# Decay by token on y instead of q, transposed rows of x in three tiles, gathers and splits earlier in each expert

## The chip, the cores and the metric

The kernel runs on one core of a Trainium2 chip. The metric is the device time of one execution in microseconds (us); smaller is better. Before the change three runs took 712.65, 709.08 and 713.63 us (median 712.65).

The engines are named as in the profile: PE is TensorE (matmuls; PEld its weight loads), DVE is VectorE, ACT is ScalarE, POOL is GpSimd, and SP is the engine whose queue issues most of the DMAs. Each engine works through its own list of instructions in order and waits where an operand isn't ready.

## The reference

Two layers follow each other. First a decaying linear attention over 4 batches, 8 heads, 768 tokens, head size 64:

```
gamma = 1 - 2 ** (-5 - head)
state = gamma * state + outer(k[t], v[t])          # one 64x64 state per batch and head
y[t]  = (q[t] @ state) / sqrt(64)
```

Its output, as 3072 rows x of 512 columns, goes through a mixture of 8 experts with two chosen per row:

```
noisy = x @ w_gate + log1p(exp(x @ w_noise)) * noise
the two largest of 8 -> softmax over these two -> weights
out[row] += weight * (relu(x[row] @ w1[e]) @ w2[e])   # w1[e]: 512x1024, w2[e]: 1024x512
```

All inputs and outputs are float32.

## The kernel before

**Attention.** The tokens are cut into 24 chunks `j` of 128 (6 per batch). Four 256 KB tiles per chunk are loaded on SP's queue: q and k with the head's dimension on the partitions, v (`in_v`) and k again (`in_kt`) with the tokens on them. The load of chunk `j + 4` is issued in the turn of chunk `j`. The decay is split into two factors: v is multiplied by gamma to a negative power of the token (`v_scale`, POOL, L328, tile `vp`), and q by gamma to the positive power times 1/sqrt(64) (`q_scale`, POOL, L336, tile `qs`; the table is `gq`). In the turn of chunk `j`, `qk(j+1)` multiplies k with `qs` (L355), `masked` puts the causal mask on it on DVE (L360, tile `am`), `y_state` (L372) and `y_mm` (L379) add up y in PSUM (`pY`), ACT copies it to SBUF (`yt`, L383), and in the next turn PE transposes it and multiplies it with the gate's weights (`x_turn`, L405). ACT copies x out of PSUM and SP writes it to `xbuf` in HBM. Between these stands the routing (DVE: `route_*`, `own_*`), which decides which rows go to which expert, and the preparation of the first expert's weights. The tables `todo`, `mid` and `first_todo` say in which chunk's turn each such step is issued.

**Precision.** The experts' matmuls run in float16 with each operand as a high and a low part, so each product takes three matmuls (L886 to L888 in the first layer, L933 to L935 in the second).

**Experts.** Each expert has a fixed capacity (`CAPS`: 832, 832, 816, 800, 800, 784, 768, 768 rows), worked in blocks of 128 rows. For each block of expert `e + 1`, while expert `e` is computed:

- `gather`: POOL issues an indirect DMA that fetches 128 rows of `xbuf` into `xg` (four buffers; L715);
- `flush`/`gate`: DVE copies the block's gate weights from `xg` (L730);
- `split`: ACT squares and sums the rows (L743), DVE works out a power of two (L746 to L748), ACT writes the high part of `xs` (L750), DVE the low part (L751; two buffers of `xs`), and SP issues a transposing DMA from `xs` into the columns of `XE[e]` (tile `xe`, L752).

The first layer, `mm1`, goes over groups of columns (rows of x): for e = 2 to 7 two halves of 416 to 384 columns, for e = 1 groups of 256, 256 and 320. In each group it runs over the 8 slices `f` of the hidden size, 12 matmuls per slice into one PSUM tile; three such tiles are in use in turn. ACT takes the high part of relu out (`hh`, L892), DVE the low part (`hl`, L895). `n` counts the slices over all groups. After the last slice `w_scale(e+1, "1")` runs, a matmul on PE (L218) over sums of squares of the next expert's `w1` that ACT has made (`w_sum`, L208, issued at the last five slices but one; `w_cast`, L214). Then come the blocks of the second layer, `mm2`, 24 matmuls of 512 columns each (a narrower tail block is packed, `mm2_tail`, L989); ACT scales the result (`ot`, L919), and POOL adds it into `out` with an indirect DMA (`put`, L924). In these blocks ACT and DVE also convert the next expert's `w1` (`w_hi` L231, `w_lo` L236).

The order on each engine is that of the program's text: the kernel is written with a manual schedule. In the second layer's loop a gather of expert `e + 1` and the put of a block take turns on POOL, and one `split` stands behind each block from the second on; the last block of `e + 1` is split at `n = 1` of expert `e + 1` itself (for e = 1 the last five blocks, at `n = 0, 2, 9, 11, 13`).

## Time and profile before

| | |
|---|---|
| runs | 712.65, 709.08, 713.63 us; median 712.65 |
| profiled execution | 709.37 us; span from its first to its last instruction 707.6 us |
| mean granted TensorE clock | 0.960 of full speed |
| PE busy | 644.0 us (91%), 5271 matmuls |
| ACT, DVE, POOL busy | 359.0, 332.2, 204.2 us |
| DMA | 113.08 MB, mean 160 GB/s |
| stages | attention to about 121 us, first expert to about 201 us, then seven experts |

How to read it: PE is the engine with the most work, so its idle stretches and its slow stretches are what can be removed. The page's busy time counts a matmul from its start to its modelled end, so matmuls overlap; the distance between the starts of two matmuls is what one costs. The granted clock is one of two levels, 2.4 GHz (1.0) or 1.2 GHz (0.5), and the mean of a stretch tells how much of it ran at the lower one.

### The profile page before, as it was taken

How to read it: one execution, taken by the hardware profiler on the slowest of the kernel's cores; microseconds unless marked ns; L12 is line 12 of the kernel's file. 1: busy time of each engine (PE TensorE's matmuls, PEld its weight loads, DVE VectorE, ACT ScalarE, POOL GpSimd, SP SyncE). 2: the span in 40 equal slices, each digit the busy share in tenths (PEclk: the TensorE clock that was granted, in tenths of full speed). 3: DMA queues.
4: the chain of work that ended last, by engine and by line, in shares of the span. 5: the costliest groups of instructions: out<-in, count | busy, mean ns of one | idle time of the engine just before them, and what ended most of it. 6: DMA issues, size and time to landing. Idle time of an engine off the chain costs nothing.

```text
span 707.6 us, 13373 instructions
## 1 busy us (share of the span) xinstructions
PE 644.0 (91%) x5271; PEld 389.3 (55%) x5271; DVE 332.2 (47%) x889; ACT 359.0 (51%) x697; POOL 204.2 (29%) x166
## 2 busy tenths in 40 slices
PE   9989769986969899799979998999699989999995
PEld 6978657555638544354435544554255446445465
DVE  4446883985337323356436234624362355246120
ACT  6444546533647337454744475547355655477121
POOL 5555650230331024201430144014400540151204
PEclk9999979998989999899989999999899999999999
DMA  9999989967347428751775176617842786186213
GB/s 314 339 368 362 363 205 297 329 150 208 77 91 195 142 43 145 107 232 31 136 115 205 44 131 125 245 30 134 117 155 94 124 136 251 31 136 91 31 15 47
DMA packets 94429, 113.08 MB, mean 160 GB/s; under 512 B 60662, under 2 KB 61820, under 8 KB 90780
## 3 DMA queue, kind: packets, MB, share of 16 engines
q1 hardware_dynamic: 82576, 85.57, 40.6%
q0 software_dynamic: 11776, 26.63, 21.3%
q8 instruction: 42, 0.69, 0.4%
q14 instruction: 23, 0.19, 0.1%
q10 hardware_dynamic: 12, 0.01, 0.0%
HBM read 72.66 MB, written 26.42 MB: 140 GB/s over the span
## 4 chain that ended last, share of the span: by engine, by line
PE 69%; DMA 14%; DVE 8%; ACT 4%; issue 3%; POOL 1%; SPq 0%; POOLq 0%; ACTq 0%; DVEq 0%
PE pH L886 11%; PE pH L887 11%; PE pH L888 11%; PE pO L933 9%; PE pO L935 9%; PE pO L934 9%; DMA xe<-xs 6%; DMA in_v<-vt 4%; DVE xs L751 2%; PE pA L355 2%; DMA xbuf<-x 2%; ACT xs L750 1%; PE pY L379 1%; ACT junk L208 1%; DMA ct<-ctab 1%
## 5 line engine op out<-in xcount | busy, mean ns | idle before, releaser
L886 PE MATMUL pH<-xe,w1h 128*128 128x384 f16 (+5 forms) x576 | 187.0, 325 | 38.9 <-DMA xe<-xs 30.5
L887 PE MATMUL pH<-xe,w1h 128*128 128x384 f16 (+5 forms) x576 | 187.1, 325 | 0.0
L888 PE MATMUL pH<-xe,w1l 128*128 128x384 f16 (+5 forms) x576 | 186.6, 324 | 0.0
L924 POOL DMA_INDIRECT out<-ot,idx x51 | 81.3, 1594 | 352.0 <-ACT ot L919 257.3
L895 DVE SCALAR_TENSOR_TENSOR hl<-pH,hh 128x384 f16<-128x384 f32 (+5 forms) x144 | 74.7, 525 | 134.4 <-ACT hh L892 133.6
L935 PE MATMUL pO<-w2h,hl 128*128 128x512 f16 x344 | 130.4, 379 | 0.0
L934 PE MATMUL pO<-w2l,hh 128*128 128x512 f16 x344 | 130.4, 379 | 0.0
L933 PE MATMUL pO<-w2h,hh 128*128 128x512 f16 x344 | 130.4, 379 | 0.0
L892 ACT ACTIVATE hh<-pH 128x384 f16<-128x384 f32 (+5 forms) x144 | 66.6, 465 | 124.7 <-PE pH L888 123.2
L886 PEld LDWEIGHTS <-w1h 128*128 128x128 f16 x576 | 58.1, 101 | 69.8 <-issue 34.0
L919 ACT ACTIVATE ot<-pO,gse 128x512 f32<-128x512 f32 x45 | 31.0, 689 | 101.9 <-PE pO L935 96.6
L887 PEld LDWEIGHTS <-w1h 128*128 128x128 f16 x576 | 57.9, 101 | 39.4 <-issue 10.0
L888 PEld LDWEIGHTS <-w1l 128*128 128x128 f16 x576 | 58.2, 101 | 33.7 <-issue 2.8
L715 POOL DMA_INDIRECT xg<-xbuf,idx x54 | 56.7, 1050 | 61.7 <-DVE idx L628 28.8
L208 ACT ACTIVATE junk<-wst 128x1024 bf16<-128x1024 f32 x64 | 67.2, 1051 | 5.9 <-DMA wst<-w 5.8
L751 DVE SCALAR_TENSOR_TENSOR xs<-xg,xup,xs 128x512 f16<-128x512 f32 (+4 forms) x54 | 45.7, 846 | 39.5 <-ACT xs L750 38.7
L935 PEld LDWEIGHTS <-hl 128*128 128x128 f16 x344 | 33.6, 98 | 40.6
L933 PEld LDWEIGHTS <-hh 128*128 128x128 f16 x344 | 33.6, 98 | 40.6 <-issue 0.4
L934 PEld LDWEIGHTS <-hh 128*128 128x128 f16 x344 | 33.6, 98 | 39.6
L750 ACT ACTIVATE xs<-xg,xup 128x512 f16<-128x512 f32 (+4 forms) x54 | 39.1, 724 | 27.8 <-DVE xup L747 24.6
L236 DVE SCALAR_TENSOR_TENSOR w1l<-wst,wsc,w1h 128x1024 f16<-128x1024 f32 x28 | 35.9, 1281 | 31.2 <-ACT w1h L231 31.2
L746 DVE TENSOR_SCALAR xp<-xss 128x1 int32<-128x1 int32 (+4 forms) x54 | 8.2, 151 | 89.6 <-ACT junk L743 89.3
(183 smaller groups left out, 787.2 us busy)
## 6 DMA issues: line engine op xcount, KB each, us to landing
wst<-w SPq DMA_DIRECT2D x28, 1024.0 KB
in_q<-qT SPq DMA_DIRECT2D x24, 256.0 KB
in_k<-kT SPq DMA_DIRECT2D x24, 256.0 KB
in_v<-vt SPq DMA_DIRECT2D x24, 256.0 KB
in_kt<-kt SPq DMA_DIRECT2D x24, 256.0 KB
xbuf<-x SPq DMA_DIRECT2D x24, 256.0 KB
out<-zero SPq DMA_DIRECT2D x6, 1024.0 KB
wst<-w SPq DMA_DIRECT2D x8, 512.0 KB
```

Of the source, the lines that this page charges most:

```text
L208: nc.scalar.activation(junk, st[:, i * 1024:(i + 1) * 1024], AF.Square, accum_out=ss[:, i:i + 1])
L715: nc.gpsimd.indirect_dma_start(out=x[:n], out_offset=None, in_=xbuf[:128 + B0 * S] if e == 0 and t < 3 else xbuf, in_offset=bass.IndirectO ...
L751: nc.vector.scalar_tensor_tensor(xs[:n, 1], x, up[:n], xs[:n, 0], op0=OP.mult, op1=OP.subtract)
L886: nc.tensor.matmul(p[:, :n], whi, xh, start=(k == 0), stop=False)
L887: nc.tensor.matmul(p[:, :n], whi, xl, start=False, stop=False)
L888: nc.tensor.matmul(p[:, :n], wlo, xh, start=False, stop=(k == KT - 1))
L892: nc.scalar.activation(hh[:, f, n0:n1], p, AF.Relu)
L895: nc.vector.scalar_tensor_tensor(hl[:, f, n0:n1], p, 0.0, hh[:, f, n0:n1], op0=OP.max, op1=OP.subtract)
L924: nc.gpsimd.indirect_dma_start(out=out, out_offset=bass.IndirectOffsetOnAxis(ap=idx[:n, i:i + 1], axis=0), in_=ot[:n], in_offset=None, com ...
L933: nc.tensor.matmul(p, a, WT["2h"][:, f, :], start=(f == 0), stop=False)
L934: nc.tensor.matmul(p, a, WT["2l"][:, f, :], start=False, stop=False)
L935: nc.tensor.matmul(p, c, WT["2h"][:, f, :], start=False, stop=(f == FT - 1))
```

## The change

- **y carries the token's factor.** `q_scale` and its tile `qs` are gone. q goes into `qk` and `y_state` as it was loaded, and where ACT copied y out of PSUM (L383), DVE now multiplies it there by the table `gq` (`yt<-pY,gq`). The table's columns are put in y's order. The buffers of q become five (three before).
- **Inputs in another order.** The first loads: v and k (`kt`) of chunk 0 come before q and k of chunk 1, and so on.
- **Weights of the first expert.** `w_sum`, `w_scale`, `w_hi` and `w_lo` of `w1` move one chunk later.
- **Three tiles for the transposed rows.** `XE[e]` becomes tiles of 384, 256 and CAPS[e] - 640 columns, and `mm1` of every expert from e = 1 on goes over these three groups (24 slices; the last group is 192 columns wide for e = 1, then 176, 160, 160, 144, 128 and 128).
- **Gathers and splits sooner.** From e = 2 on the first four gathers of `e + 1` are issued at `n = 9, 11, 13, 15` and the first four splits at `n = 13, 15, 17, 19`, the other three of each at the second layer's blocks 0 to 2 and 1 to 3. For e = 1: gathers at `n = 13, 15, 17, 19`, splits at `17, 19, 21, 23`. At the end of e = 0 three blocks are split, not two; the others in e = 1 at `n = 0, 2, 9, 11`.

```diff
     for h in range(H):
-        y[h % 2, h // 2, :] = gamma[h] ** (p + 1.0) / math.sqrt(D)
-        g[h % 2, :, h // 2] = gamma[h] ** (np.arange(NC) * float(C))
+        o, x = (h // 2 + h % 2) % 2, h % 2 * 2 + h // 4
+        y[o, x, :] = gamma[h] ** (p + 1.0) / math.sqrt(D)
+        g[o, :, x] = gamma[h] ** (np.arange(NC) * float(C))
     rest, parts = np.concatenate([y.reshape(2, HP * C), g.reshape(2, NC * HP)], 1).astype(np.float32), []
...
             IN[n, j] = loads.tile([128, HP, C] if n in "kq" else [128, DM], F32, name="in_" + n,
-                                  bufs=AHEAD + {"k": 0, "q": -1, "v": 0, "kt": 1}[n])
+                                  bufs=AHEAD + {"k": 0, "q": 1, "v": 0, "kt": 1}[n])
             nc.sync.dma_start(IN[n, j].rearrange("p a c -> p (a c)") if n in "kq" else IN[n, j], src[n][j])
...
     nc.sync.dma_start(cs, ctab[:, :SOON])
+    load(0, ("v", "kt"))
     load(1, "qk")
-    load(0, "v")
-    load(2, "q")
-    load(0, ("kt",))
-    load(2, "k")
     nc.sync.dma_start(wgf, wgn)
-    load(1, ("v", "kt"))
+    load(1, ("v",))
+    load(2, "qk")
+    load(1, ("kt",))
+    load(2, ("v", "kt"))
     for j in range(3, AHEAD):
-        load(j, "qk")
-        load(j - 1, ("v", "kt"))
-    load(AHEAD - 1, ("v", "kt"))
+        load(j)
...
-    VP, AM, QS, PY, PT, YT, LG = {}, {}, {}, {}, {}, {}, {}
+    VP, AM, PY, PT, YT, LG = {}, {}, {}, {}, {}, {}
     pctx = ExitStack()
...
-    def q_scale(j):
-        QS[j] = loads.tile([128, HP, C], F32, name="qs", bufs=3)
-        eng, m = nc.vector if j == 0 else nc.gpsimd, 2 if j < 2 else 1
-        for x in range(m):
-            r = slice(x * HP // m, (x + 1) * HP // m)
-            eng.tensor_tensor(QS[j][:, r], IN["q", j][:, r], gq[:, j % NC].rearrange("p (a c) -> p a c", a=HP)[:, r], op=OP.mult)
-
     def q_table(c):
...
-    q_scale(0)
     q_table(1)
...
                 nc.tensor.matmul(pA[s][:, i, :], IN["k", j][r, i, :],
-                                 QS[j][r, i, :], start=True, stop=True)
+                                 IN["q", j][r, i, :], start=True, stop=True)
         return pA
...
                 r = slice(s * 64, s * 64 + 64)
-                nc.tensor.matmul(yplace(j, i, s), U[c % 2][r, i, :], QS[j][r, i, :],
+                nc.tensor.matmul(yplace(j, i, s), U[c % 2][r, i, :], IN["q", j][r, i, :],
                                  start=(i < 2), stop=False, skip_group_check=True)
...
         y = YT[j].rearrange("p s g c -> p (s g c)")
-        nc.scalar.activation(y.rearrange("p (s x) -> p s x", s=2), PY.pop(j)[:, :, :2 * C], AF.Copy)
+        nc.vector.tensor_tensor(y.rearrange("p (s x) -> p s x", s=2), PY.pop(j)[:, :, :2 * C],
+                                gq[:, c].rearrange("p (s x) -> p s x", s=2), op=OP.mult)
         if c < NC - 1:
...
         o, n, i = block(e, t)
-        if t == 0:
-            XE[e] = XP[e % 2].tile([128, 2 * KT, CAP], F16, name="xe")
+        if t in (0, 3, 5):
+            w = {0: FIRST, 3: 640 - FIRST, 5: CAP - 640}[t]
+            XE[e, o] = XP[e % 2].tile([128, 2 * KT, w], F16, name=f"xe{t}")
         x = XP[0].tile([128, XROW], F32, name="xg", bufs=4)
...
             nc.vector.scalar_tensor_tensor(xs[:n, 1], x, up[:n], xs[:n, 0], op0=OP.mult, op1=OP.subtract)
-            nc.sync.dma_start_transpose(XE[e][:, :, o:o + n], xs[:n].rearrange("p a d -> p (a d)"))
+            b = (0, FIRST, 640)[(t >= 3) + (t >= 5)]
+            nc.sync.dma_start_transpose(XE[e, b][:, :, o - b:o - b + n], xs[:n].rearrange("p a d -> p (a d)"))
...
         at((4, 6, 9, 12)[i], w_load, 0, "1", i)
-        at0((6, 8, 11, 14)[i], w_sum, 0, "1", i)
-        at0(15 + i, w_hi, 0, "1", i)
+        at0((7, 9, 12, 15)[i], w_sum, 0, "1", i)
+        at0(16 + i, w_hi, 0, "1", i)
         at((20, 20, 21, 21)[i], w_load, 0, "2", i)
...
             at0(22 + i, w_sum, 0, "2", i)
-    first_todo[15].insert(0, (w_scale, (0, "1")))
-    for i, j in ((0, 16), (1, 16), (2, 17), (3, 17), (4, 18), (5, 19), (6, 20), (7, 21)):
+    first_todo[16].insert(0, (w_scale, (0, "1")))
+    for i, j in ((0, 17), (1, 17), (2, 18), (3, 18), (4, 19), (5, 20), (6, 20), (7, 21)):
         P(j, w_lo_half, 0, "1", i)
...
-    q_scale(1)
     v_scale(0)
...
             f(*a)
-        if j < 2:
-            q_scale(j + 2)
         if more:
             v_scale(j + 1)
-        if 2 <= j < NCH - 2:
-            q_scale(j + 2)
         if more:
...
             wlo = WT["1l"][:, k, f * 128:(f + 1) * 128]
-            xh, xl = XE[e][:, k, n0:n1], XE[e][:, KT + k, n0:n1]
+            xh, xl = XE[e, n0][:, k, :n], XE[e, n0][:, KT + k, :n]
             nc.tensor.matmul(p[:, :n], whi, xh, start=(k == 0), stop=False)
...
     for e in range(E):
-        half = (CAPS[e] + 31) // 32 * 16
-        cols = [(FIRST, 640), (640, CAPS[0])] if e == 0 else [(0, half), (half, CAPS[e])]
-        if e == 1:
-            cols = [(0, 256), (256, 512), (512, CAPS[e])]
+        cols = [(0, FIRST), (FIRST, 640), (640, CAPS[e])][not e:]
         n, more = 0, e + 1 < E
...
         for n0, n1 in cols:
-            if n0 and ready:
+            if n0 == FIRST and ready:
                 for t in range(ready):
...
                 mm1(e, n0, n1, f)
-                if n in ((2, 4) if e == 0 else (0, 2, 9, 11, 13) if e == 1 else (1,)):
+                if n in ((2, 4) if e == 0 else (0, 2, 9, 11, 17, 19, 21, 23) if e == 1 else (13, 15, 17, 19)):
                     split()
+                if e and ahead and n in ((13, 15, 17, 19) if e == 1 else (9, 11, 13, 15)):
+                    ahead.pop(0)()
+                    flush(2)
                 if e:
...
                     w_sum(e + 1, "2", n - 2)
-            if more and (n in (1, 2) if e == 0 else n):
+            if more and 0 < n < 4:
                 split()
```

The order of the instructions moves at three places. The first is ACT at the end of expert 3's first layer, before the change (`hh` is the high part of relu, `junk,wss` a sum of squares of the next expert's `w1`, `wsb` what `w_scale` on PE waits for):

```order
L892 ACTIVATE hh<-pH 128x400 x5
L208 ACTIVATE junk,wss_4536<-wst_4535 128x1024
L892 ACTIVATE hh<-pH 128x400
L208 ACTIVATE junk,wss_4536<-wst_4535 128x1024
...
L214 ACTIVATE wsb_4740<-wss_4536 128x4
L892 ACTIVATE hh<-pH 128x400
```

The same place now, all slices of the third group of columns (`junk,xss` and `xs` are the two ACT instructions of a split):

```order
L881 ACTIVATE hh<-pH 128x160 x2
L736 ACTIVATE junk,xss<-xg 128x512
L743 ACTIVATE xs<-xg,xup 128x512
L881 ACTIVATE hh<-pH 128x160 x2
L736 ACTIVATE junk,xss<-xg 128x512
L743 ACTIVATE xs<-xg,xup 128x512
L209 ACTIVATE junk,wss_4614<-wst_4613 128x1024
L881 ACTIVATE hh<-pH 128x160
...
L215 ACTIVATE wsb_4994<-wss_4614 128x4
L881 ACTIVATE hh<-pH 128x160
```

The four sums of squares still stand at the last slices but one; those slices are 160 columns wide now, not 400, and two of the four splits that moved forward stand before them in the same group.

The second place is DVE around chunk 15 of the attention, where the lists of the first rows are made; now (`yt<-pY,gq` is y times its table, `am` the masked scores of the next chunk, `a` and `ob` one-hot tables of the routing):

```order
L374 TENSOR_TENSOR yt<-pY,gq 128x512
L351 TENSOR_TENSOR am<-pA,mask 128x512 x2
L549 TENSOR_TENSOR a_12_1269<-lanes,lf_12_1267 128x1536
L557 TENSOR_TENSOR ob_12_1335<-blks,lf_12_1267 128x84
L559 TENSOR_TENSOR ob_12_1335<-ob_12_1335,tokn 128x84
L530 COPY cum<-pR 128x9
L531 TENSOR_SCALAR cum<-cum 128x1
L374 TENSOR_TENSOR yt<-pY,gq 128x512
L351 TENSOR_TENSOR am<-pA,mask 128x512 x2
```

Each chunk's `yt` now stands on DVE behind the routing of its turn and ahead of the next chunk's mask; before, DVE had the same rows without `yt`, and the four small instructions of `w_scale` after the two rows of `cum`.

The third place is POOL in expert 4, now (`xg<-xbuf` is a gather, `out<-ot` a put):

```order
L708 DMA xg<-xbuf,idx 128x528 x5
L913 DMA out<-ot,idx 3200x512
L708 DMA xg<-xbuf,idx 128x528
L913 DMA out<-ot,idx 3200x512
L708 DMA xg<-xbuf,idx 16x528
L913 DMA out<-ot,idx 3200x512 x5
```

Before, one gather and one put took turns through all seven blocks of the second layer. Now four gathers are through before the first put.

## Rows read from the trace of the kernel before

**Rows 1.** Busy time by engine in two stretches of the attention (columns as in the first row).

```profile
core 0: us, PE busy (x) PEld busy (x) DVE busy (x) ACT busy (x) POOL busy (x), PEclk, DMA share, GB/s
60.00:80.00 20.00, 15.26 (x318) 13.93 (x322) 17.58 (x54) 8.31 (x21) 11.64 (x9) 0.94 1.03 358
80.00:100.00 20.00, 14.79 (x336) 12.93 (x330) 17.00 (x30) 9.65 (x20) 13.98 (x12) 0.93 0.78 268
```

**Rows 2.** Groups by line and shape: busy us, mean ns | idle before.

```profile
L360 DVE TENSOR_TENSOR am<-pA,mask 128x512 f32<-128x512 f32 x48 | 30.9, 686 | 34.0 <-PE pA L355 34.0
L336 POOL TENSOR_TENSOR qs<-in_q,gq 128x512 f32<-128x512 f32 x22 | 28.4, 1292 | 31.1 <-DMA in_q<-qT 17.8 <-PE pY L372 9.5 <-PE pU L388 3.8
```

**Rows 3.** Timeline, all engines, about 91 us: start, duration, instruction.

```profile
91.46 1.05 POOL L328 TENSOR_TENSOR vp<-in_v,cs 128x512 f32<-128x512 f32 x1
91.63 5.87 DVE L751 SCALAR_TENSOR_TENSOR xs<-xg,xup,xs 128x512 f16<-128x512 f32 x1 [0.73 <-ACT xs L750]
...
95.91 1.03 POOL L328 TENSOR_TENSOR vp<-in_v,cs 128x512 f32<-128x512 f32 x1
```

**Rows 4.** Groups by line on PE: 275 to 600 us, then 195 to 245 us.

```profile
L886 PE MATMUL pH<-xe,w1h 128*128 128x400 f16 (+2 forms) x307 | 105.3, 343 | 21.0 <-DMA xe<-xs 14.1 <-issue 5.0 <-DVE hl L895 1.9
L886 PE MATMUL pH<-xe,w1h 128*128 128x256 f16 (+1 forms) x86 | 25.6, 298 | 10.6 <-DMA xe<-xs 10.5
```

**Rows 5.** Timeline of PE: two resumptions, idle time before them in brackets.

```profile
234.71 0.43 PE L886 MATMUL pH<-xe,w1h 128*128 128x320 f16 x1 [3.08 <-DMA xe<-xs]
...
581.28 0.32 PE L886 MATMUL pH<-xe,w1h 128*128 128x384 f16 x1 [1.95 <-DVE hl L895]
```

**Rows 6.** Ten us behind each resumption (columns as in rows 1).

```profile
207.30:217.30 10.00, 10.00 (x77) 8.29 (x78) 4.19 (x16) 4.79 (x11) 4.91 (x4) 0.83 0.52 80
234.70:244.70 10.00, 9.99 (x62) 6.70 (x63) 1.97 (x4) 2.80 (x7) 0.00 (x0) 0.83 0.51 201
288.70:298.70 10.00, 10.00 (x47) 5.04 (x48) 3.97 (x13) 3.49 (x7) 2.46 (x2) 0.80 0.61 102
361.90:371.90 10.00, 9.99 (x43) 4.98 (x44) 3.23 (x10) 3.82 (x9) 2.74 (x3) 0.71 0.58 102
433.10:443.10 10.00, 10.00 (x52) 5.43 (x52) 6.46 (x17) 4.53 (x10) 4.05 (x4) 0.85 0.56 93
506.50:516.50 10.00, 9.97 (x47) 5.19 (x48) 3.83 (x12) 3.96 (x9) 2.37 (x2) 0.77 0.44 89
581.30:591.30 10.00, 10.00 (x62) 6.05 (x62) 6.89 (x19) 6.18 (x9) 1.57 (x2) 1.00 0.80 266
```

**Rows 7.** Timeline of ACT, expert 0, slices of 192 columns with sums of squares.

```profile
180.34 1.06 ACT L208 ACTIVATE junk<-wst 128x1024 bf16<-128x1024 f32 x1
...
181.39 0.33 ACT L892 ACTIVATE hh<-pH 128x192 f16<-128x192 f32 x1
181.60 1.07 ACT L208 ACTIVATE junk<-wst 128x1024 bf16<-128x1024 f32 x1
```

**Rows 8.** Timeline of ACT, expert 1: from a split's first instruction to what follows it.

```profile
224.09 0.62 ACT L743 ACTIVATE junk<-xg 128x512 bf16<-128x512 f32 x1
...
225.84 0.37 ACT L892 ACTIVATE hh<-pH 128x256 f16<-128x256 f32 x1
```

**Rows 9.** Timeline, end of expert 2's first layer: `wsb` and the matmul behind it.

```profile
323.52 0.21 ACT L214 ACTIVATE wsb<-wss 128x4 bf16<-128x4 f32 x1
...
323.78 0.17 PE L218 MATMUL pR<-wsb,oneb 128*128 128x4 bf16 x1
```

**Rows 10.** Timeline of PE at the full clock: narrow matmuls, each with its own weight load.

```profile
177.41 0.32 PE L619 MATMUL pB<-ob,a 128*128 128x49 f16 x6
177.57 0.24 PE L886 MATMUL pH<-xe,w1h 128*128 128x192 f16 x1
...
178.06 0.25 PE L886 MATMUL pH<-xe,w1h 128*128 128x192 f16 x1
```

**Rows 11.** The chain of waits into expert 1: start, duration, what.

```profile
201.59 5.56 DMA xe<-xs
```

**Rows 12.** Timeline of DVE behind expert 0's last block.

```profile
203.20 0.75 DVE L993 SCALAR_TENSOR_TENSOR ot<-pT,gse,ot 64x512 f32<-64x512 f32 x1
```

## The prediction

> **What bounds the kernel now.** I read the busy times by stretch first, then the groups by line with their idle time, then the timeline where idle time is large, and last the order of ACT's instructions, because PE's waits end there. In the attention's middle the DMAs are full (share 1.03 from 60 to 80 us, 0.78 from 80 to 100) while DVE has hardly any room left (17.58 and 17.00 of 20 us) [rows 1]. So the input's volume sets the pace first and DVE's queue later; POOL and ACT have room. In the experts PE is the bound, and what can be won is its idle time ahead of the first layer: 21.0 us between 275 and 600 us, mostly waits for transposed rows, and 10.6 us around expert 1 [rows 4]. Idle time costs twice. Behind each of the longer waits the clock ran at the lower of its two levels for a while: in the ten us behind the four large waits between experts the mean was 0.80, 0.71, 0.85 and 0.77, so 2.0, 2.9, 1.5 and 2.3 us were lost, 8.7 in all [rows 6]. A wait of 1.95 us had no such cost (1.00 behind it), one of 3.08 us had (0.83) [rows 5, 6].
>
> **The waits between experts, e = 2 to 7.** The gathers and splits of the next expert now start in the first layer. The last split of `e + 1` stands behind block 3 of the seven of `e`, so three blocks of some 5 us lie between it and the first use. The whole wait goes, and with it the slow stretch: -21.0 - 8.7 = **-29.7 us**. Next in line there would be the conversion of `w1`, which is through a block or more earlier as before. The bound on the other side is that nothing goes, if the transposes are late all the same (a rival).
>
> **What ACT has to do now in the third group.** This is the price. The moved splits bring two ACT instructions each into the first layer. In the second group (256 columns) there is room. In the third the slices are 128 to 192 columns wide, and the four sums of squares of the next `w1`, tied to the last slices, stand there too. One sum of squares with one `hh` takes ACT 1.26 us, of which `hh` 0.21 [rows 7], so 1.05 without it. A split holds ACT 1.75 us from its first instruction to the next `hh`, its wait for DVE included [rows 8]. From the start of the third group in e = 2 to 6 ACT has: the `hh` and split of the slice before, 2.0; seven `hh`, some 1.4; two splits, 3.5; four sums, 4.2; and 0.26 from `wsb` to the matmul behind it [rows 9]. That is 11.4 us. PE cannot pass: `w_scale` waits on `wsb` and stands ahead of the whole second layer, and only three PSUM tiles let the slices run ahead of ACT. PE alone needs less: matmuls of 192 columns follow each other in 0.49 / 6 = 0.082 us [rows 10], which is 192 columns at 2.4 GHz and 2 ns, so 8 x 12 of them cost 7.2 us at 176 columns, 6.6 at 160, 6.0 at 144 and 5.3 at 128. The waits: 4.2, 4.8, 4.8, 5.4, 6.1, together 25.3. For e = 1 (192 columns, 7.9 us) there is no split just before, but three stand ahead of `wsb`: 2.1 for two slices, six `hh` 1.3, splits 5.25, sums 4.2 and 0.26 make 13.1, so 5.2. In all **+30.5 us**. The lower bound is half of it, if PE could use part of the wait; the upper bound adds up to 1 us per expert, because `xs` has two buffers and the third split must wait for the first one's transpose (5.56 us where others were in flight [rows 11]).
>
> **The clock behind these waits.** Each wait falls into pieces: about 2 us while PE lacks a PSUM tile, another 1, and some 2.4 before `w_scale`. One such piece lies at or above the 1.95 us that cost nothing and below the 3.08 us that cost 1.7 [rows 5, 6], but three of them stand close together. Bounds 0 and six times 1.7, 10; I take **+5**.
>
> **Expert 1's first wait.** Its first group is now 384 wide, not 256, so it needs a third block, whose split stands behind the packed tail block of expert 0. DVE finishes that tail at 203.20 + 0.75 = 203.95 [rows 12]; then come the power of two, 0.3, ACT's and DVE's part of `xs`, about 0.75 each, and a transpose of 5.56 [rows 11]: 211.3 us, where before the second block had landed at 201.59 + 5.56 = 207.2. That is +4.2. Against it the wait of 3.08 us in the middle goes, with its 1.7 of slow clock, as the last two splits stand two slices sooner and the group ahead of them is longer: **-0.6**.
>
> **More matmuls.** e = 2 to 7 have 96 more each, 576 at 2 ns: **+1.2**. At this point a row and a rule differ. Six matmuls of 49 columns, each with a load of 128x128 weights, took 0.16 us, 27 ns each [rows 10], so a weight load does not hold back a matmul of 128 columns at 55 ns. The Trainium skill (TensorE: Matmul & The Clock Gate, Back-to-back issue gap) says that a sustained stream of load and matmul pairs takes about 81 ns each at 128 columns. By that rule expert 7, where ACT has nothing else beside it, would pay, as an estimate, 96 x 26 ns = 2.5 us more, and the others nothing, since 96 x 81 ns = 7.8 us still hides behind ACT's 11.4.
>
> **Attention.** POOL loses 22 multiplies of 1.29 us [rows 2], ACT its copy; neither bounds. DVE gets 24 multiplies out of PSUM, priced like the mask, 0.69 us [rows 2]. From 60 to 80 us five of them, 3.4 us, meet 17.58 busy: 1 us over [rows 1]. In the turns with splits DVE has mask 1.3, y 0.7, two low parts of weights 1.5 and a split 1.2, 4.7 us for a turn of some 4: three turns, +2. Against it stands one instruction of DVE that took 5.87 us, not the 0.75 of its like [rows 3, 12], while POOL ran vp and `qs` without a break beside it; without `qs` there is no such run: -5.1. Sum **-2**; bounds -7 (all of y's multiplies hidden) and +8 (the stall stays on account of vp, and every y from chunk 12 on counts). The order of the first loads and the five q buffers I cost at nothing: the DMAs carry the same bytes, and nothing there waits for a q buffer.
>
> **Sum.** -29.7 + 30.5 + 5 - 0.6 + 1.2 - 2 = +4.4 on the profiled execution's 709.4: 713.8. The median shown, 712.65, lies 3.3 above that execution, so the same sum on it gives 717. I predict **715**.
>
> **Rivals.** *Even (the forecast, 0.48)*: the waits between experts move into the third group; its own range is 707 to 722.
>
> *Faster (0.2).* The clock stays up behind the pieces of wait (-5) and the attention gains its whole stall (-5 more): 704 to 707. For it: no piece alone reaches 3.08 us. Against it: DVE's 17 of 20 us [rows 1].
>
> *Slower through the clock (0.2).* The pieces act as one wait, and the slow stretch behind each is as long as the longest of rows 6, 2.9 us: six times 2.9 in place of 5 is +12.4, 726 to 729. Its place is the end of each first layer from e = 1 to 6, and it decides from the point where the pieces count like the 3.08 us of rows 5. The Trainium skill (TensorE: Matmul & The Clock Gate, A second HAM failure mode: psum-queue depth-cycling) describes a kernel in which short idle times between matmul groups, one PSUM tile after another, kept the clock going down and up. By that rule this case is the likely one; the 1.95 us with no cost speaks against it here, so I leave it at 0.2.
>
> *Slower in the attention (0.08).* DVE becomes its bound and the term is +8, not -2: 724.
>
> *The waits stay (0.04).* If the transposes queue behind the 2 MB of `w2` on SP, -29.7 falls away: 744. Against it: four of seven stand ahead of those loads, and the last has three blocks of time.
>
> **Chances and range.** One per cent, 7 us, is about what a measurement of this kernel can tell from no change. Faster by more than that (below 705.5): most of the faster rival, 0.17. Slower (above 719.8): both slower rivals, the last one and the forecast's upper edge, 0.31. Between: 0.52. The range from 701 to 728 leaves out the last rival and the tails of the others.
>
> **What would show it.** Right: no idle ahead of the first matmul of e = 2 to 7; in each third group of e = 1 to 6 PE waits 4 to 6 us, in part for ACT's `hh`, in part at `w_scale` for `wsb`; expert 1 starts later than before against the end of expert 0; no DVE instruction of 5 us near 92 us; POOL below 180 us busy. Wrong: if PE passes the third group in its own 5 to 8 us, the main price is wrong and the time falls to about 685; if the attention ends later than before, DVE's queue was underrated.

## The result and the profile after

The changed kernel takes **721.0 us** (720.0 to 722.3), the kernel before 711.1 beside it: a ratio of **1.014, 95% interval 1.009 to 1.018**. The profiled execution took 722.29 us, with a span of 720.5; before it was 709.37. The forecast was 715 in a range of 701 to 728. The time lies in the range, but above the one per cent within which I had put 0.52 of the chance: it belongs to the 0.31 for slower.

The page after: the span, each engine's busy time, and the granted clock in 40 slices of 18 us.

```profile
span 720.5 us, 14594 instructions
PE 647.5 (90%) x5847; PEld 422.6 (59%) x5847; DVE 340.5 (47%) x959; ACT 349.5 (49%) x721; POOL 174.8 (24%) x142
PEclk9999889998979999999999899989999999899999
```

The groups by line on PE answer to [rows 4]. First 195 to 245 us, then 275 to 600, then `L875` and the matmul of `w_scale` (`L219`) from 240 to 650 us, which holds all six third groups.

```profile
L875 PE MATMUL pH<-xe,w1h 128*128 128x384 f16 (+2 forms) x96 | 28.0, 292 | 10.2 <-DMA xe<-xs 9.1 <-DVE hl L884 1.1
...
L875 PE MATMUL pH<-xe,w1h 128*128 128x384 f16 (+4 forms) x435 | 119.7, 281 | 12.8 <-DVE hl L884 12.7
...
L875 PE MATMUL pH<-xe,w1h 128*128 128x384 f16 (+6 forms) x488 | 130.8, 276 | 17.4 <-DVE hl L884 17.2
L219 PE MATMUL pR<-wsb,oneb 128*128 128x4 bf16 x11 | 1.8, 166 | 15.4 <-ACT wsb L215 15.4
```

The 21.0 us of waiting between experts are gone: what ends the idle time now is `hl`, not a transpose. In their place stand 17.4 us for `hl` and 15.4 in front of `w_scale`. Expert 3's third group shows how they fall, first in PE's timeline, from the group's first matmul on (the idle time before each in brackets):

```profile
382.94 0.23 PE L875 MATMUL pH<-xe,w1h 128*128 128x160 f16 x1
...
386.41 0.23 PE L875 MATMUL pH<-xe,w1h 128*128 128x160 f16 x1 [0.70 <-DVE hl L884]
388.67 0.23 PE L875 MATMUL pH<-xe,w1h 128*128 128x160 f16 x1 [0.44 <-DVE hl L884]
393.42 0.23 PE L875 MATMUL pH<-xe,w1h 128*128 128x160 f16 x1 [2.92 <-DVE hl L884]
396.79 0.16 PE L219 MATMUL pR<-wsb,oneb 128*128 128x4 bf16 x1 [1.72 <-ACT wsb L215]
```

and in ACT's timeline, with the fourth split (the second in this group), two of the four sums and the end:

```profile
388.39 0.20 ACT L736 ACTIVATION_READ_ACCUMULATOR junk<-xg 128x1 f32 x1
391.06 0.72 ACT L743 ACTIVATE xs<-xg,xup 128x512 f16<-128x512 f32 x1 [2.47 <-DMA xe<-xs]
391.69 1.04 ACT L209 ACTIVATE junk<-wst 128x1024 bf16<-128x1024 f32 x1
392.72 0.28 ACT L881 ACTIVATE hh<-pH 128x160 f16<-128x160 f32 x1
392.91 1.04 ACT L209 ACTIVATE junk<-wst 128x1024 bf16<-128x1024 f32 x1
...
396.54 0.20 ACT L215 ACTIVATE wsb<-wss 128x4 bf16<-128x4 f32 x1
```

ACT's one long break, beside waits for DVE of 0.4 and 0.6 us in the splits, is 2.47 us in the middle of the fourth split, when it waits for an earlier transpose to give back one of the two `xs` buffers. The `hh` that PE needs stands behind both.

The ten us behind each of the six `w_scale` matmuls answer to [rows 6] (stretch, length, busy time and instructions of PE, PEld, DVE, ACT and POOL, granted clock, DMA share, GB/s).

```profile
247.00:257.00 10.00, 10.00 (x41) 4.20 (x41) 3.35 (x12) 3.23 (x6) 1.77 (x2) 0.84 0.68 210
321.30:331.30 10.00, 10.00 (x40) 4.21 (x40) 8.85 (x35) 1.82 (x3) 1.70 (x2) 0.83 0.41 169
396.80:406.80 10.00, 10.00 (x40) 4.20 (x40) 2.01 (x8) 1.86 (x3) 1.61 (x1) 0.82 0.41 170
469.70:479.70 10.00, 10.00 (x35) 3.95 (x35) 0.96 (x8) 1.80 (x3) 0.83 (x1) 0.71 0.41 172
544.30:554.30 10.00, 10.00 (x41) 4.19 (x41) 2.18 (x8) 1.78 (x3) 1.97 (x2) 0.86 0.44 171
616.90:626.90 10.00, 10.00 (x36) 3.99 (x36) 1.13 (x8) 1.78 (x3) 1.04 (x1) 0.73 0.42 175
```

PE works through every one of these stretches, and in each the clock stood at 1.2 GHz for 3 to 6 us: 1.6 + 1.7 + 1.8 + 2.9 + 1.4 + 2.7 = 12.1 us lost. In expert 3 the slow stretch begins before its window and costs 0.8 more, so 13.

In the attention, the windows that answer to [rows 1], the split that answers to the 5.87 us of [rows 3], and the group of y's new multiplication; then two waits of PE, the first in the kernel before (in front of `w_scale` of expert 0), the second in the changed one:

```profile
60.00:80.00 20.00, 18.44 (x429) 16.35 (x428) 17.06 (x63) 8.45 (x20) 4.16 (x4) 1.00 1.02 333
80.00:100.00 20.00, 13.38 (x286) 12.05 (x288) 15.43 (x48) 8.80 (x21) 8.25 (x9) 0.83 1.08 329
...
94.99 0.83 DVE L744 SCALAR_TENSOR_TENSOR xs<-xg,xup,xs 128x512 f16<-128x512 f32 x1 [0.73 <-ACT xs L743]
...
L374 DVE TENSOR_TENSOR yt<-pY,gq 128x512 f32<-128x512 f32 x24 | 16.5, 689 | 12.2 <-PE pY L370 9.3 <-ACT lgs L408 2.2 <-issue 0.6
...
77.16 0.18 PE L218 MATMUL pR<-wsb,oneb 128*128 128x4 bf16 x1 [3.75 <-DMA xbuf<-x]
...
89.81 1.34 PE L397 MATMUL pT<-turn,yt 64*64 64x80 f32 x32 [4.77 <-DVE yt L374]
```

DVE is busy for less of both stretches than before, although the multiplication is its own now; the stretches don't hold quite the same chunks, and the long instruction lay in the second only. The gain does not arise where that instruction stood. The 17th `yt` starts at 75.57 us, before the change at 82.64: 7.1 sooner already, with PE's wait of 3.75 us gone (its `w_scale` stands a chunk later now) and the three one-hot instructions of DVE beside it taking 2.2 us in all, not 4.6. Two turns later PE waits 4.77 us for DVE's `yt`, and the lead is down to 2.5 (88.98 against 91.50). Behind the long instruction it is 6.2 (95.75 against 101.90), and 5.1 at expert 0's first product.

### The profile page after: what moved, and what is told of

Read it like the earlier page. It is cut to its first block, busy times and chain, and to the rows that moved or that the text cites. A ratio compares the mean times of both kernels' runs of the same rounds, so it can differ in the third digit from the quotient of the medians.

```text
span 720.5 us, 14594 instructions
## 1 busy us (share of the span) xinstructions
PE 647.5 (90%) x5847; PEld 422.6 (59%) x5847; DVE 340.5 (47%) x959; ACT 349.5 (49%) x721; POOL 174.8 (24%) x142
## 4 chain that ended last, share of the span: by engine, by line
PE 61%; DMA 17%; ACT 7%; DVE 7%; issue 5%; SPq 1%; POOL 1%; POOLq 0%; ACTq 0%
PE pO L922 10%; PE pO L923 10%; PE pO L924 10%; PE pH L875 9%; PE pH L877 9%; PE pH L876 9%; DMA xe<-xs 5%; DMA in_k<-kT 4%; ACT junk L209 4%; DMA xbuf<-x 3%; DMA in_v<-vt 2%; DVE xs L744 2%; ACT xs L743 2%; PE pT L978 1%; DMA xg<-xbuf,idx 1%
## 5 line engine op out<-in xcount | busy, mean ns | idle before, releaser
L875 PE MATMUL pH<-xe,w1h 128*128 128x384 f16 (+6 forms) x768 | 209.5, 280 | 34.0 <-DVE hl L884 18.9
L876 PE MATMUL pH<-xe,w1h 128*128 128x384 f16 (+6 forms) x768 | 209.6, 280 | 0.0
L877 PE MATMUL pH<-xe,w1l 128*128 128x384 f16 (+6 forms) x768 | 209.4, 280 | 0.0
L884 DVE SCALAR_TENSOR_TENSOR hl<-pH,hh 128x384 f16<-128x384 f32 (+6 forms) x192 | 80.7, 433 | 127.2 <-ACT hh L881 125.4
L922 PE MATMUL pO<-w2h,hh 128*128 128x512 f16 x344 | 135.6, 394 | 0.0
L923 PE MATMUL pO<-w2l,hh 128*128 128x512 f16 x344 | 135.2, 393 | 0.0
L881 ACT ACTIVATE hh<-pH 128x384 f16<-128x384 f32 (+6 forms) x192 | 73.4, 388 | 117.0 <-PE pH L877 102.9
L876 PEld LDWEIGHTS <-w1h 128*128 128x128 f16 x768 | 75.9, 99 | 41.4 <-issue 22.8
L875 PEld LDWEIGHTS <-w1h 128*128 128x128 f16 x768 | 75.9, 99 | 38.1 <-issue 12.1
L877 PEld LDWEIGHTS <-w1l 128*128 128x128 f16 x768 | 76.0, 99 | 20.2 <-issue 0.9
L744 DVE SCALAR_TENSOR_TENSOR xs<-xg,xup,xs 128x512 f16<-128x512 f32 (+4 forms) x54 | 40.7, 754 | 44.3 <-ACT xs L743 44.3
L327 POOL TENSOR_TENSOR vp<-in_v,cs 128x512 f32<-128x512 f32 x24 | 25.3, 1054 | 65.1 <-DMA in_v<-vt 50.4
```

The costliest lines, as they stand in the source:

```text
L744: nc.vector.scalar_tensor_tensor(xs[:n, 1], x, up[:n], xs[:n, 0], op0=OP.mult, op1=OP.subtract)
L875: nc.tensor.matmul(p[:, :n], whi, xh, start=(k == 0), stop=False)
L876: nc.tensor.matmul(p[:, :n], whi, xl, start=False, stop=False)
L877: nc.tensor.matmul(p[:, :n], wlo, xh, start=False, stop=(k == KT - 1))
L881: nc.scalar.activation(hh[:, f, n0:n1], p, AF.Relu)
L884: nc.vector.scalar_tensor_tensor(hl[:, f, n0:n1], p, 0.0, hh[:, f, n0:n1], op0=OP.max, op1=OP.subtract)
```

## The experiments

The kernels ran in four groups, each on one chip beside the kernel before, whose median there was 701.7 us (x1, x8, x6, x3), 707.6 (a2, x9, c1, c2), 703.8 (x4, c6, c5) and 705.8 (c7). So ratios to it are compared between groups, not times. The forecasts in us of the first group (x1, x8, x6, x3) were made from the 711.1 us of the first result; as ratios they are these times divided by 711.1.

**x1: the sums of squares sooner.**

```
-if more and e and len(cols) * FT - 5 <= n < len(cols) * FT - 1:
-    w_sum(e + 1, "1", n - (len(cols) * FT - 5))
+s0 = 13 if e == 1 else 8
+if more and e and s0 <= n < s0 + 4:
+    w_sum(e + 1, "1", n - s0)
```

> Edit: in experts 1 to 6 the four sums of squares over the next expert's first weights stand earlier: behind slices 8 to 11 of 24 (13 to 16 in expert 1) and no longer behind slices 19 to 22, where ScalarE also makes the four splits and the narrow slices' results. Theory (ScalarE's pile-up in the third column group, and the half clock behind it, are what ate the gain): TensorE's waits in the third groups fall from 32.8 us in sum to 5 to 10, the half-clock stretches behind them (about 12 us by the stages) go nearly all: 683 to 693 us against 721 of the changed kernel. Rival 1 (the third, narrow group itself, its matmuls and weight loads, costs the time): the waits for hh and hl stay, 715 to 722. Rival 2 (the sums only move their 5 us per expert onto the second group, where the splits now begin): as much wait in front of the middle group's slices, 710 to 722.

Measured: 692.1 us, ratio 0.987 (0.981 to 0.993). PE from 240 to 650 us:

```profile
L875 PE MATMUL pH<-xe,w1h 128*128 128x384 f16 (+6 forms) x531 | 143.5, 278 | 14.8 <-DVE hl L884 14.6
L219 PE MATMUL pR<-wsb,oneb 128*128 128x4 bf16 x12 | 2.0, 168 | 0.0
```

The waits at `w_scale` go whole and moving the sums onto the second group cost nothing, so neither rival holds. But the ratio misses the theory's 0.960 to 0.975 too, and 14.8 us for `hl` stay, more than the 5 to 10 that I gave: ACT still waits 1.1 to 2.4 us for a transpose in the last splits of experts 2 to 6. Of the six slow stretches one is left.

**x8: gathers and splits where they were, three tiles kept.**

```
-if n in (... (0, 2, 9, 11, 17, 19, 21, 23) if e == 1 else (13, 15, 17, 19)):
+if n in (... (0, 2, 9, 11) if e == 1 else (1,)):
     split()
-if e and ahead and n in (...):
-    ahead.pop(0)()
-    flush(2)
...
-if more and 0 < n < 4:
+if more and (0 < n < 4 if e == 0 else n):
     split()
```

> Edit: the three tiles and three column groups stay, but from expert 1 on the gathers and splits stand where the kernel before has them (gathers and splits among the blocks of the second product; expert 1's own splits behind slices 0, 2, 9 and 11). Theory (the three tiles alone take away the wait for the last transposes at each expert's start; the earlier splits alone load ScalarE in the third group): third-group waits fall to below 10 us in sum, no idle of over 1 us in front of the first matmul of experts 2 to 7: 680 to 692 us. Rival 1 (it is the earlier gathers and splits that took the wait at the start away): the waits at the starts return, some 3 us at each expert, and the time is 700 to 712. Rival 2 (sums and narrow slices alone are too much for ScalarE in the third group): 710 to 722.

Measured: 701.7 us, ratio 0.998 (0.993 to 1.002). That is outside the theory's range (0.956 to 0.973 as a ratio) and inside that of rival 1 (0.984 to 1.001), but not by rival 1's mechanism. PE from 240 to 650 us:

```profile
L875 PE MATMUL pH<-xe,w1h 128*128 128x384 f16 (+6 forms) x515 | 139.0, 279 | 8.6 <-DVE hl L884 8.4
L219 PE MATMUL pR<-wsb,oneb 128*128 128x4 bf16 x12 | 2.0, 166 | 12.1 <-ACT wsb L215 12.1
```

No matmul of experts 2 to 7 waits for a transpose at its start, so the three tiles with their column groups alone take that wait away; the earlier splits weren't needed for it. The 8.4 us for `hl` lie in the first group, behind late splits in which ACT waits 0.7 to 2.3 us for a gather, and the sums in the narrow slices alone are worth 12.1 us at `w_scale`.

**x6: `w_scale` behind the first block of the second product.** Edit: the line `w_scale(e + 1, "1")` moved from ahead of that loop to behind its first `put`.

> Edit: the broadcast product of w_scale for the next expert's first weights, TensorE's instruction that waits for the last sum of squares, stands behind the first block of the second product and no longer ahead of it. Theory (the in-order queue of TensorE makes the sums' lateness its own wait): the six waits in front of that product (3.98, 2.31, 1.72, 2.38, 2.45 and 2.52, 15.4 us in sum) go, with half or all of the half clock behind them (6 to 12 us); the waits for hl in the third group (17 us) stay: 693 to 703 us. Rival (what is late behind it is the next step of the same chain, the halves of the next expert's weights at the end of the second product, and the next expert's first slice waits for them): 712 to 721.

Measured: 695.6 us, ratio 0.992 (0.988 to 0.996). The same two groups show 17.4 us for `hl`, as after the change, and 0.0 at `L219`: the theory's waits, and no next one behind them. The ratio lies just above the forecast's 0.975 to 0.989. In the traces the stretch from expert 1's first matmul to the span's end takes 490.9 us, after the change 516.2: 25.3 less, of which 15.4 are the waits and some 9.5 the clock, for two slow stretches (3.4 us each) are left there of the six, which cost 13. By the ratios the gain is 15 us against the first result and 21 against a2 below.

**x3 and x4: the change's two halves, each on the kernel before.** x3 takes the diff's parts up to `y_mm`, the loads' order and expert 0's later weight steps; x4 the parts from `gather` on and the column groups.

> Edit: the kernel before with the attention part of the change alone: decay on y in VectorE, no scaled q, inputs in the new order, expert 0's weight steps one chunk later; experts as before. Theory (the attention gained 5 us, as the start of expert 0's first product shows, 113.2 against 118.3 us, and the experts lost the rest): 704 to 708 us, 3 to 7 below the kernel before. Rival (VectorE's multiplication, late behind others, costs as much in a normal run, and the 5 us are one execution's chance): 710 to 714.

> Edit: the kernel before with the expert part of the change alone (three tiles and column groups, earlier gathers and splits); attention, inputs and expert 0's weight steps as before. Theory (attention gains some 4 us, as x3 showed with a ratio of 0.9944, and the experts lose more than the whole result: pile-up and half clock against the waits between experts): the ratio to the kernel before is that of the changed kernel (1.014 to 1.022) plus 0.005: 1.017 to 1.030. Rival (the two parts are not independent: y's product in VectorE is also what delays the experts): 1.000 to 1.012.

Measured: x3 698.1 us, ratio 0.994 (0.990 to 0.999); x4 728.8 us, ratio **1.037** (1.032 to 1.042), above even the theory's 1.030. So the attention gained and the experts lost, 25 us by x4's median. In the traces the stretch from expert 1's first matmul to the span's end takes 500.3 us before the change and 495.6 in x3, whose experts are the same; 516.7 in x4, and 516.2 and 516.6 in the two traces of the changed kernel. So the experts' loss is 16 to 21 us with either attention, and x4's rival falls. The two halves don't add up, though: 0.994 times 1.037 is 1.031, and the whole change has 1.014 and 1.022. x4's extra time lies ahead of expert 1, which starts at 209.7 us there, at 207.3 before, and at 204.3 and 200.5 in the changed kernel; how much of it is the chip stays open. In the two traces with the old attention (before, x4) the first product of expert 0 starts at 118.3 and 117.8 us, in the twelve with the new one at 109.0 to 113.2, mean 110.9: a gain of 7, where the pair that I read first gave 5.1.

**a2: the change again.** No edit.

> The changed kernel itself once more, because x1, x3, x6 and x8 ran on a chip on which the kernel before takes 701.7 us and not 711: its ratio to the kernel before there is needed beside theirs. If its 1.0138 is the change's own, the ratio is 1.008 to 1.018, its third-group waits sum to 30 to 35 us again, and all six are followed by a half-clock stretch. If instead the third-group waits cost the clock less on this chip than in the first execution (in x6, on that chip, only two of six waits for hl were followed by one), the ratio is 0.995 to 1.007.

Measured: 719.7 us, ratio 1.022 (1.014 to 1.029). The waits are the same (16.9 for `hl`, 14.8 at `w_scale`), and all six have a slow stretch behind them. The loss is the change's own. Why it is 1.014 on one chip and 1.022 on the other isn't settled; the waits that the change removes differ too (31.6 us ahead of the first products from 195 us on in the first trace of the kernel before, 26.1 in x3).

**x9: the waits filled.**

```
+def fill(e, n):
+    for _ in range(FILL.get((e, n), 0)):
+        nc.tensor.matmul(pR[:, :FIRST], WT["1h"][:, 0, :128], XE[e, 0][:, 0, :FIRST], ...)
...
+                fill(e, n)
                 mm1(e, n0, n1, f)
...
+            fill(e, 24)
             w_scale(e + 1, "1")
```

> Edit: the changed kernel with extra products of 384 columns (0.16 us each) whose result nobody reads, put in front of the third-group slices and of the w_scale products at which TensorE was seen to wait over 1 us, each batch shorter than the wait it stands in: 20.5 us of TensorE's idle filled, no wait taken away. Theory (the half clock behind the six waits is a cost of its own, some 12 us in the changed kernel's trace): the half-clock stretches at the end of the third groups go, all or nearly all, the waits' ends stay where they were, and the time is 6 to 13 us below the changed kernel's in the same call. Rival (the waits alone are the cost, and the half clock runs while TensorE has to wait anyhow): within 3 us of the changed kernel, or above it by what the extra products overrun.

Measured: 709.2 us, ratio 1.004 (1.000 to 1.008), 10.5 us below a2. PE's groups from 240 to 650 us (`L1094` is the filling), and three of the six windows behind `w_scale`, the others alike:

```profile
L875 PE MATMUL pH<-xe,w1h 128*128 128x384 f16 (+6 forms) x513 | 138.5, 278 | 8.4 <-DVE hl L884 8.2
L1094 PE MATMUL pR<-xe,w1h 128*128 128x384 f16 x137 | 24.4, 326 | 0.0
L219 PE MATMUL pR<-wsb,oneb 128*128 128x4 bf16 x12 | 2.0, 166 | 2.6 <-ACT wsb L215 2.5
...
246.90:256.90 10.00, 10.00 (x48) 4.57 (x48) 3.35 (x12) 3.21 (x6) 2.63 (x2) 1.00 0.69 201
463.00:473.00 10.00, 9.71 (x48) 4.43 (x46) 2.24 (x9) 2.84 (x6) 2.32 (x2) 1.00 0.54 202
606.80:616.80 10.00, 10.00 (x48) 4.58 (x48) 2.16 (x8) 1.82 (x3) 2.63 (x2) 1.00 0.56 187
```

137 useless products of 0.16 us were added, 22 us of work, and the kernel got faster: the clock reads 1.00 behind all six. No wait was taken away, only filled: from a third group's first matmul to the `w_scale` matmul behind it the six experts take 77.2 us in sum, 78.1 in a2. From expert 1's first matmul to the span's end it takes 503.4 us against 516.6 in a2: 13.2 us, about what the six half-clock stretches cost there (14.1). The rival falls.

**c1: everything early.** Splits behind slices 5, 7, 8 and 10, sums behind 9, 11, 12 and 13, gathers behind 1 to 4, for experts 2 to 6 (the copies of the gate weights, `flush`, move with them).

```
-(13, 15, 17, 19)     +(5, 7, 8, 10)      split
-(9, 11, 13, 15)      +(1, 2, 3, 4)       gather
+sums = (13, 14, 15, 16) if e == 1 else (9, 11, 12, 13)
```

> Edit: in experts 2 to 6 all work for the next expert stands in the first two column groups: gathers behind slices 1 to 4, splits behind 5, 7, 8 and 10, sums of squares behind 9, 11, 12 and 13 (expert 1: sums behind 13 to 16, the rest as changed). Theory (only what ScalarE must do in the third group costs anything there): the third-group waits fall to below 4 us in sum, from some 33 in the changed kernel and 13 to 16 in x1, with no wait at the experts' starts either: 6 to 13 us below x1, a ratio of 0.968 to 0.980 to the kernel before. Rival (ScalarE or VectorE is then late in the first two groups, for hl): as x1, 0.983 to 0.992.

Measured: 727.9 us, ratio **1.034** (1.026 to 1.041). The theory falls, and the rival's range is left far behind too, though its mechanism is what is seen: PE waits 41.9 us in this group, 14.8 in x1. That line (240 to 650 us), two of PE's waits in expert 4's second group, and ACT's instructions there:

```profile
L875 PE MATMUL pH<-xe,w1h 128*128 128x384 f16 (+6 forms) x483 | 131.5, 282 | 41.9 <-DVE hl L884 26.9 <-DVE xp L739 14.9
...
456.58 0.27 PE L875 MATMUL pH<-xe,w1h 128*128 128x256 f16 x1 [1.00 <-DVE xp L739]
459.89 0.27 PE L875 MATMUL pH<-xe,w1h 128*128 128x256 f16 x1 [1.85 <-DVE xp L739]
...
454.32 0.62 ACT L736 ACTIVATE junk<-xg 128x512 bf16<-128x512 f32 x1
454.84 0.19 ACT L736 ACTIVATION_READ_ACCUMULATOR junk<-xg 128x1 f32 x1
456.80 0.72 ACT L743 ACTIVATE xs<-xg,xup 128x512 f16<-128x512 f32 x1 [1.77 <-DVE xup L740]
457.43 0.36 ACT L881 ACTIVATE hh<-pH 128x256 f16<-128x256 f32 x1
```

A split goes from ACT to DVE and back. With low parts of weights in DVE's queue (1.28 us each) it held ACT 3.1 us here, not the 1.75 of [rows 8], and a slice of 256 columns takes PE 1.3.

**c2: c1 with expert 0's border mended.** The load of expert 1's second weights (2 MB) stands behind slice 3 of expert 0's second group, not ahead of it; its splits behind slices 1 and 3; expert 1's first three splits before, behind, and before the second of expert 0's last blocks.

> Edit: c1, and around expert 0: the load of expert 1's second weights (2 MB) behind slice 3 of expert 0's second group and no longer ahead of it, the splits there behind slices 1 and 3, and expert 1's first three splits ahead of, behind, and ahead of the second of expert 0's blocks of the second product. Theory: the wait in front of expert 0's third group (7.4 us in x1, where a transpose issued at 157.2 us landed 11.7 us later beside 4 MB of weights) falls to 2 to 4, the one in front of expert 1 (8.65 us in x1, its third split behind two results and a gather's copy) to 0 to 3, with part of the half clock behind them (10 us of it behind each in x1, at a loss of 5): 10 to 18 us below c1. Rival (the transposes wait for something else that ends as late, the gathers' landings or expert 1's weight parts): 0 to 4 us below c1.

Measured: 713.1 us, ratio 1.011 (1.004 to 1.018), 15 below c1, as the theory said. PE's group from 155 us on, c1 first (to 210 us), then c2 (to 200):

```profile
L875 PE MATMUL pH<-xe,w1h 128*128 128x192 f16 (+2 forms) x56 | 16.4, 293 | 15.2 <-DMA xe<-xs 14.9 <-DVE hl L884 0.3
...
L875 PE MATMUL pH<-xe,w1h 128*128 128x192 f16 (+2 forms) x67 | 18.8, 281 | 2.0 <-DMA xe<-xs 1.2 <-DVE hl L884 0.5 <-DVE xp L739 0.3
```

**c6 (x1 with c2's steps) and c5.** c5 is x8 with x1's sums and c2's steps, and with an expert's last three splits behind slices 1, 5 and 7 of its own first group (gate copies and output scales move with them).

```
-(0, 2, 9, 11) if e == 1 else (1,)       +(0, 2, 9, 11) if e == 1 else (1, 5, 7)
-(0 < n < 4 if e == 0 else n)            +(n == 0 if e == 0 else 0 < n < 5)
```

> Edit: x1 (sums of squares early, splits as changed) with c2's steps around expert 0 (second weights' load behind a slice, splits one slice sooner, expert 1's first three splits around the first blocks). Theory: x1's ratio of 0.987 less the 15 us that the same steps took off between c1 and c2: 0.962 to 0.972. Rival (the steps only gained there because c1 had other waits behind them): 0.980 to 0.988.

> Edit: x8 (gathers and splits among the blocks of the second product) with x1's early sums, with the last three of the seven splits of an expert moved from the end of the second product to behind slices 1, 5 and 7 of the first group, where ScalarE has room between two results of 384 columns, and with c2's steps around expert 0. Theory (a piece of ScalarE's work costs nothing where TensorE's slice is longer than that piece and the slice's own result together, 1.92 us a slice in the first group against 1.28 in the second): no wait of over 1 us in experts 2 to 6, 0.945 to 0.962. Rival (the last splits still wait for gathers that land late, as at 420.4 us in x8, and hold up hh): 0.962 to 0.975, no better than c6.

Measured: c6 672.6 us, ratio **0.957** (0.952 to 0.962), better than forecast. PE's group from 240 to 650 us, and the stretch from 190 to 640:

```profile
L875 PE MATMUL pH<-xe,w1h 128*128 128x384 f16 (+5 forms) x576 | 153.0, 275 | 13.7 <-DVE hl L884 13.6
...
190.00:640.00 450.00, 434.69 (x2964) 264.92 (x2963) 202.41 (x548) 250.21 (x495) 116.65 (x87) 1.00 0.56 128
```

The waits for `hl` in the third groups are nearly those of x1, and the clock stays whole behind all of them.

c5 took 670.4 us, ratio **0.954** (0.948 to 0.960). Its time is in the theory's range, but not its picture: at the border of the first two groups PE waits 2.65 us for `hl` in four experts, for DVE's share of the seventh split and the output scales.

**c7: c5 with the seventh split and the scales a little later.** Split behind slice 9, scales behind 10, sums behind 11 to 14.

> Edit: c5 with the seventh split of experts 2 to 6 behind slice 9 and no longer behind slice 7, the output scales (three short VectorE operations that need it) behind slice 10, and the sums of squares behind slices 11 to 14. Theory (the 2.65 us that TensorE waits for hl at the border of the first two groups in experts 2 to 5 of c5 is VectorE's queue: a split's part, the scales, and the last low part of the second weights, all between slices 7 and 8): these waits and the 3.4 us half-clock stretch behind three of them go, 10 to 15 us below c5, 0.930 to 0.942 of the kernel before. Rival (the same work in the shorter slices of the second group makes the same wait there, as in c1): 0.950 to 0.962, as c5.

Measured: 659.5 us, ratio **0.944** (0.937 to 0.952): just above the forecast's 0.942, and below c5 by 0.010, some 7 us, not 10 to 15. It beats both kernels. Three things moved at once in c7, so which of them counts isn't shown.

```profile
L875 PE MATMUL pH<-xe,w1h 128*128 128x384 f16 (+5 forms) x576 | 152.4, 276 | 0.5
...
200.00:300.00 100.00, 99.36 (x720) 65.19 (x719) 52.64 (x149) 57.72 (x117) 20.64 (x16) 1.00 0.58 144
300.00:400.00 100.00, 99.90 (x645) 56.80 (x644) 45.19 (x120) 61.28 (x116) 33.42 (x27) 1.00 0.66 136
400.00:500.00 100.00, 99.80 (x742) 64.15 (x741) 48.31 (x125) 58.97 (x120) 20.89 (x17) 1.00 0.59 146
500.00:600.00 100.00, 99.89 (x649) 57.12 (x647) 46.55 (x120) 63.35 (x120) 28.94 (x22) 1.00 0.65 129
```

From 240 to 650 us the group waits 0.5 us where it waited 17.4, and the clock is whole throughout. ACT and DVE do the same work as in the changed kernel; only its order differs.

## Why the prediction came out as it did

- **Waits between experts, -29.7: right.** Not one is left at the start of experts 2 to 7, nor the slow stretch behind. x8 adds that the three tiles with their column groups do this alone. The size is that of one execution: in x3, with the same experts, these waits sum to 16.2 us, not 21.0.
- **ACT in the third group, +30.5: right in place, 8 too small.** PE's rows show 17.4 + 15.4 = 32.8, in the two kinds foretold; x1 and x6 take the `w_scale` part away and x8 most of the other. But from the third group's first matmul to `w_scale` the six experts take 13.5, 12.7, 13.8, 12.4, 13.0 and 12.5 us (expert 3: 382.94 to 396.79), 38.2 more than PE's own work as I reckoned it. The sums of ACT's work, 13.1 and five times 11.4, were good: in the last five ACT waits 1.2, 2.5, 1.0, 1.8 and 1.3 us for an `xs` buffer, 7.7 in all, and without that they are 11.2 to 11.5. I had that wait only as a bound, up to 1 us per expert, and left it out. That 30.5 comes so near the 32.8 of the rows is luck: the rows leave out some 0.16 us of every wait (see below).
- **The clock behind these waits, +5 with 10 as the bound: this step failed.** It cost 13. I priced the pieces singly and took them for half harmless, because 1.95 us had cost nothing [rows 5, 6]. Standing close together they were followed by a slow stretch all six times, in both traces of the changed kernel. That is the mechanism of the rival to which I gave 0.2, and x9 shows it as a cost of its own: 13.2 us with the waits still there. The Trainium skill (TensorE: Matmul & The Clock Gate, A second HAM failure mode: psum-queue depth-cycling), which I had set aside for that one row, describes this; the trace of the changed kernel agrees. Waits of this kind are not always followed by one, though: with those for `hl` alone it was two of six in x6, one in x1, none in c6.
- **Expert 1's first wait, -0.6: right within 2 us.** The wait grew from 6.34 to 8.54 us, not by 4.2, its slow stretch by 0.7; the wait in the middle fell from 3.08 to 0.53, and its 1.7 went. A wait of 1.10 at 221.0 us, which the term left out, went too: -2.4 in all.
- **More matmuls, +1.2: the term holds, something beside it was missing.** In the third group of expert 6 matmuls of 128 columns start 0.056 us apart, as reckoned, and so they do in expert 7, for which the estimate by the other rule was 2.5 us more. But from expert 1 on PE's time without idle time and clock loss grew by 4.2 us (500.3 less 25.4 and 13.1 before, 516.2 less 33.5 and 16.7 now). The view counts idle time from the modelled end of the last matmul (0.22 us for 128 columns), so each wait costs some 0.16 more than its row says; 25 waits in place of 8 make 2.8 of it.
- **Attention, -2: right in sign, too small, and not by its mechanism.** -5.1 in the profiled execution, -7 over all traces, 4 by x3's median. That the first is just what the long DVE instruction lost is luck: 7.1 us were won ahead of it, most of them in a turn from which expert 0's `w_scale` went, a step that my sum does not have. PE's 4.77 us for `yt` give most of that back: `yt` stands behind a split in DVE's queue there, and DVE itself waits 2.46 us for ACT, which waits 2.81 for a gather. I had priced DVE's busy time, at 3, and not this. No run tests the load order, the q buffers and the moved weight steps apart from y's multiplication, so the shares stay open.

In sum the clock's cost was underrated by 8 us and the waits in the third groups by 8, the attention's gain by 3 to 5 and that at expert 1 by 2: the errors offset in part, and the kernel came out slower by 10 us, not by 2.5 (by 12.9, not 4.4, between the two profiled executions). The rival's 726 to 729 had put the clock at 17.4, 4 too much, and no more gain in the attention than the forecast.

## What to carry to other kernels

For small waits that follow each other closely, a slow stretch behind each group of them should stand in the sum's upper bound in full, even if each wait alone has cost nothing elsewhere; whether that cost is real can be tried by filling the waits with useless products. Where helper work for the next stage stands counts as much as how much of it there is: the same instructions in the orders of c2, c5 and c7 gave ratios of 1.011, 0.954 and 0.944. A piece that goes through another engine and back is to be priced with that engine's queue (3.1 us in c1, not 1.75) and with the buffers that it must get back. And a tile split by consumer can take away a wait that an earlier issue was meant to take away.

## What the runs showed of the hardware

The half clock did not follow from a wait's length alone. In c5 three of four equal waits of 2.64 or 2.65 us were followed by a slow stretch and one was not (the ten us behind the second and the third):

```profile
351.00:361.00 10.00, 9.99 (x90) 8.57 (x90) 3.06 (x8) 4.29 (x12) 0.00 (x0) 0.85 0.56 210
420.80:430.80 10.00, 10.00 (x111) 9.31 (x111) 3.68 (x10) 4.67 (x13) 0.00 (x0) 1.00 0.56 211
```

In x6, waits of 0.84, 1.79 and 1.11 us in expert 5 had none behind them, and 0.98, 0.69 and 1.93 in expert 6 had one. In c6 waits of up to 2.53 us, 13.7 us in all, had none at all. What decides between such cases stays open.

A transpose's time depends on what is in flight: beside the loads of expert 1's weights, transposes issued at 157.2 and 163.2 us in x1 landed after 11.7 and 6.3 us; in c2, with half of these loads behind them, the same two, issued at 152.7 and 156.9, took 6.4 and 2.9.
